# Chunked attention and a four-expert mixture: three groups of 1024 tokens in halves of 512 in place of four of 768, half expert steps, and an order searched over a moving stretch

## The chip, the cores and the metric

The kernel runs on one core of a Trainium2 chip. The metric is the device time of one execution in microseconds; before the change it was 1044.03 us (median of three runs, 1043.26 to 1044.74). Engines are named as in the profile: PE is the matrix engine, PEld its weight loads, DVE the vector, ACT the scalar and POOL the GpSimd engine; SP issues the DMAs.

## The reference, cut to what matters

Attention in chunks of 32 queries, each with 16 keys to the left, 8 to the right and 8 memory slots, is followed by four experts that all tokens visit; their results are weighed by normalised probabilities and added.

```python
B, H, S, D = 4, 8, 768, 64          # q, k, v; 3072 tokens of H * D = 512 in all
for c in range(S // 32):
    q_c = q[:, :, 32*c : 32*c+32]
    k_full = concat([mem_k, k[:, :, l:r]])      # l, r: 16 to the left, 8 to the right
    v_full = concat([mem_v, v[:, :, l:r]])
    a = exp(s - max(s)), s = q_c @ k_full.T / 8
    out[chunk] = a / (sum(a) + 1e-9) @ v_full
x = out.transpose(0, 2, 1, 3).reshape(3072, 512)
p = probs / (probs.sum(-1) + 1e-9)
for e in range(4):                   # w1: 512 x 1024, w2: 1024 x 512
    y += p[:, e] * (relu(x @ w1[e]) @ w2[e])
```

## The kernel before

**Number format.** A wide product is made of three matmuls in a 32-bit format that PE rounds (fp32r): each operand is split into a `hi` part, rounded by ACT, and a `lo` part, the rest, by DVE or POOL (`parts_of`). hi x hi, lo x hi and hi x lo are added in PSUM.

**Groups.** The 3072 tokens go through the experts in four groups of 768, in two halves of `SG` = 384 columns (one batch element each, b = 0 to 3); `n` = 4 b + e counts expert steps. Attention works on units of 96 queries, 8 to a group. The opening makes the units of the first group; those of the next group are strewn into the steps before it (`attend`, `window`). A unit has three pieces on PE: scores (`S`, L485), the turn of the probabilities (`T`, L1350, in the opening alone; later DVE transposes them in blocks, L661) and the product with v (`X`, L1369 and L618).

**The layers.** The first expert of the first group has plain products (`plain_first`, L817). All other first layers go by a scheme with seven products in place of eight (Strassen's, with sums of weight blocks and of token blocks made beforehand; `Pair`, `product`, L883): a pair p of blocks of 128 hidden rows takes the products 1, 2, 6, 5, 7, 4, 3 with SG columns and 6 matmuls each. There are four pairs to an expert (`NP2`). The second layer is made in three ways. Group 0 (`Tokens`, L863) multiplies 128 tokens with 512 columns of w2, eight hidden blocks of three matmuls to a bank. Group 1 (`Halves`, L1123) has the seven products with 256 columns. Groups 2 and 3 (`Across`, L1167) have the seven products with outputs across: 128 output features by 384 tokens, two strips, four pairs of three matmuls to a bank. After each bank, DVE (ACT the first time) adds it to an accumulator in SBUF (`add_up`, `join`).

**Weights.** While group 0 is worked on, the sums of w1 blocks (`make_pair`) and of w2 blocks (`make2_combined`, half of them later) are made and written to DRAM; from group 1 on, a ring of 9 buffers (`Stream`) reads them back, 30 transfers to an expert step. At a change of group, `combine_x` makes the sums of token blocks, 4 subtractions and 7 splits.

**Order.** Nothing is scheduled by the compiler. The program records operations with what they read and write (`Plan.add`); the order of PE is that in which they are recorded. The recorded order of the opening is the text `FIRST_BLOCK` (`W` n: n idle matmuls that keep PE's clock up, `S` u, `T` u, `X` u: unit u; `M` f, `N` f: hidden block f for the first units or for the rest of the half; `g`, `G`: a token tile's second layer). There are three plans: opening, group 0 (`plan.run(ahead=LEAD)`) and the rest. `Plan.run` then orders the other engines in a list scheduler with due times: it tries `TURNS` shifts of due times over the whole plan, chooses between DVE and POOL (or ACT and DVE) where an operation has two ways, and keeps what its own cost formulas call shortest.

## Time and profile before

| | |
|---|---|
| reported time, median of 3 runs | 1044.03 us |
| profiled execution, first to last instruction | 1041.7 us |
| DVE busy | 809.4 us (78%), 1358 instructions |
| ACT busy | 539.3 us (52%), 1426 |
| POOL busy | 464.9 us (45%), 426 |
| DMA moved | 300.88 MB, mean 289 GB/s |
| granted PE clock | 0.997 of full speed on average |

Of the profiled execution only the span is recorded; the median of the three runs is 2.3 us above it. A row of the grouped view gives the busy time of a group and the mean of one instruction. For PE that mean is from issue to modelled end and overlaps the next matmul, so the rate of PE is read from long rows of the chain (time of the row divided by its count) or from start to start.

### The profile page before, as it was taken

Reading aid. Unit: us, or ns where it says so; the run is one execution under the profiler, and the core shown is the slowest. Engines: PE = TensorE matmul, PEld = TensorE weight load, DVE = VectorE, ACT = ScalarE, POOL = GpSimd, SP = SyncE. Lnnn points to the kernel's source line nnn. Section 1 sums busy time; section 2 is a strip of 40 time slices with the busy share of each in tenths; the row PEclk is TensorE's granted clock in tenths of the full one; section 3 lists DMA queues with packets and bytes.
Section 4 is the critical chain, followed back from the end, with each engine's and each line's share of the span. In section 5 each row is a group of like instructions: output and inputs, shape, how many; then the busy total and the mean of one; then the engine's idle time right before and its main releaser. Section 6 shows DMA issues by size and latency. Waiting matters only on the chain.

```text
span 1041.7 us, 21404 instructions
## 1 busy us (share of the span) xinstructions
PE 1030.7 (99%) x7899; PEld 988.8 (95%) x7899; DVE 809.4 (78%) x1358; ACT 539.3 (52%) x1426; POOL 464.9 (45%) x426
## 2 busy tenths in 40 slices
PE   7999999999999999999999999999999999999998
PEld 6988988989889999999999999999999999999998
DVE  6869786868976768678797968969699765949485
ACT  5636864746737656474755546445453534334241
POOL 2444654854605436172253606346072634626172
PEclk8999999999999999999999999999999999999999
DMA  9557989989979999999988878879679887879784
GB/s 297 179 206 238 376 335 359 357 333 352 347 279 384 357 306 333 326 342 328 309 259 303 282 259 278 279 246 296 232 241 305 287 262 247 280 237 275 250 253 144
DMA packets 185512, 300.88 MB, mean 289 GB/s; under 512 B 14816, under 2 KB 125504, under 8 KB 185408
## 3 DMA queue, kind: packets, MB, share of 16 engines
q1 hardware_dynamic: 185408, 299.51, 84.4%
q8 instruction: 63, 1.03, 0.4%
q14 instruction: 41, 0.34, 0.1%
HBM read 230.21 MB, written 69.26 MB: 287 GB/s over the span
## 4 chain that ended last, share of the span: by engine, by line
PE 93%; DVE 4%; DMA 1%; issue 1%; POOL 0%; ACT 0%; SPq 0%; DVEq 0%; POOLq 0%; ACTq 0%
PE a_ps L883 22%; PE moe_ps L883 16%; PE moe_ps L863 13%; PE a_ps L1167 12%; PE moe_ps L1167 10%; PE a_ps L1123 7%; PE moe_ps L1123 5%; PE moe_ps L817 3%; PE x_ps L618 2%; PE s_ps L485 2%; DVE A_lo L568 1%; DVE u L983 1%; DVE u L568 1%; DMA raw<-in_w_dram 1%; DMA qk_pair<-in_qk_dram 1%
## 5 line engine op out<-in xcount | busy, mean ns | idle before, releaser
L569 POOL TENSOR_TENSOR u<-u,routes 128x384 f32<-128x384 f32 x46 | 50.3, 1095 | 191.8 <-ACT u L552 191.5
L568 DVE TENSOR_TENSOR A_lo<-u,A_hi 128x384 fp32r<-128x384 f32 x139 | 118.2, 868 | 18.8 <-ACT A_hi L550 18.4
L863 PE MATMUL moe_ps<-w,h_hi 128*128 128x512 f32 x384 | 119.8, 393 | 0.0
L568 DVE TENSOR_TENSOR u<-moe_ps,u 128x384 f32<-128x384 f32 x120 | 66.2, 552 | 63.4 <-PE moe_ps L883 48.3
L569 POOL TENSOR_TENSOR raw<-raw 128x256 f32<-128x256 f32 x57 | 51.2, 899 | 127.1 <-DMA raw<-in_w_dram 83.1
L550 ACT COPY u<-a_ps 128x384 f32<-128x384 f32 x120 | 57.0, 475 | 78.8 <-PE a_ps L883 77.1
L550 ACT CAST A_hi<-u 128x384 fp32r<-128x384 f32 x144 | 73.3, 514 | 37.5 <-DVE u L983 31.1
L863 PEld LDWEIGHTS moe_ps<-w,h_hi 128*128 128x128 f32 x384 | 71.1, 188 | 14.8
L883 PE MATMUL a_ps<-xc_hi,ring 128*128 128x384 f32 x384 | 82.2, 336 | 0.0
L552 ACT ACTIVATE u<-u 128x384 f32<-128x384 f32 x96 | 50.2, 525 | 53.3 <-DVE u L568 52.7
L863 PE MATMUL moe_ps<-w,h_lo 128*128 128x512 f32 x192 | 75.0, 391 | 0.0
L569 POOL TENSOR_TENSOR us<-u,u 128x384 f32<-128x384 f32 x43 | 49.4, 1149 | 41.8 <-DVE u L983 20.3
L883 PEld LDWEIGHTS a_ps<-xc_hi,ring 128*128 128x128 f32 x384 | 67.8, 188 | 0.0
L1167 PE MATMUL a_ps<-A_hi,ring 128*128 128x384 f32 x256 | 65.8, 338 | 0.6 <-DVE u L983 0.6
L569 POOL TENSOR_TENSOR us<-u,us 128x384 f32<-128x384 f32 x43 | 49.5, 1151 | 30.2 <-DVE us L568 23.7
L569 POOL TENSOR_TENSOR u<-u,u 128x384 f32<-128x384 f32 x48 | 59.8, 1246 | 0.6
L569 POOL TENSOR_TENSOR u<-u,us 128x384 f32<-128x384 f32 x46 | 58.2, 1266 | 2.7 <-DVE A_lo L568 1.1
L639 ACT ACTIVATE s_sb<-s_ps,mx 96x64 f32<-96x64 f32 x192 | 57.1, 309 | 0.7
L568 DVE TENSOR_TENSOR acc<-a_ps,acc 128x384 f32<-128x384 f32 x52 | 28.8, 553 | 26.7 <-PE a_ps L1167 26.1
L883 PE MATMUL a_ps<-xc_lo,ring 128*128 128x384 f32 x192 | 48.9, 336 | 0.0
L1167 PEld LDWEIGHTS a_ps<-A_hi,ring 128*128 128x128 f32 x256 | 45.8, 188 | 2.4 <-DVE u L983 2.2
L569 POOL TENSOR_TENSOR w<-raw,w 128x512 fp32r<-128x512 f32 x25 | 35.9, 1443 | 26.7 <-ACT w L550 17.6
(237 smaller groups left out, 3110.8 us busy)
## 6 DMA issues: line engine op xcount, KB each, us to landing
ring<-k SPq DMA_DIRECT2D x144, 512.0 KB, 4.8
ring<-t SPq DMA_DIRECT2D x96, 512.0 KB, 6.0
ring<-w SPq DMA_DIRECT2D x72, 512.0 KB, 5.4
k<-w SPq DMA_DIRECT2D x48, 512.0 KB, 5.3
w<-w SPq DMA_DIRECT2D x32, 512.0 KB, 5.5
raw<-in_w_dram SPq DMA_DIRECT2D x62, 256.0 KB, 5.2
ring<-k SPq DMA_DIRECT2D x48, 256.0 KB, 4.1
qk_t<-in_qk_dram SPq DMA_DIRECT2D x24, 464.0 KB, 6.3
```

The source lines that it names most:

```text
L485: nc.tensor.matmul(s_ps.ap[c * CH:(c + 1) * CH, j * NPAIR + g, 0:KW], lhsT=x()[rows, g * UQ + c * CH:g * UQ + (c + 1) * CH], rhs=x()[rows, ...
L550: nc.scalar.copy(out(), x())
L552: nc.scalar.activation(out(), x(), func)
L568: ("DVE", t_dve(cols), lambda: nc.vector.tensor_tensor(out=out(), in0=x(), in1=y(), op=op)),
L569: ("POOL", t_pool(cols), lambda: nc.gpsimd.tensor_tensor(out=out(), in0=x(), in1=y(), op=op)),
L618: nc.tensor.matmul(x_out()[j * D:(j + 1) * D, g, :], lhsT=v_t.ap[:, h * D:(h + 1) * D], rhs=aT[:, j * NPAIR + g, :], start=True, stop=True,)
L639: now["plan"].add("ACT", t_act(KW) + 0.08, lambda h=h: nc.scalar.activation(s_sb.ap[:, h, :], s_in()[:, h, :], AF.Exp, bias=mx.ap[:, h, :] ...
L817: nc.tensor.matmul(ps.ap[:, lo:hi], lhsT=a[:, c * P:(c + 1) * P], rhs=x[:, c, lo:hi], start=(i == 0), stop=(i == len(steps) - 1),)
L863: nc.tensor.matmul(self.ps.ap, lhsT=h.ap[:, self.rows], rhs=w.ap[:, part, :], start=(i == 0 and k == 0), stop=(i == NF - 1 and k == 2),)
L883: nc.tensor.matmul(ps.ap[:, 0:SG], lhsT=a()[:, c * P:(c + 1) * P], rhs=y[:, k0 + c, :], start=(first and i == 0), stop=(i == len(steps) - ...
L1123: nc.tensor.matmul(ps.ap[:, cols], lhsT=x.ap[:, rows], rhs=w_ap[:, y, :], start=(begins and k == 0 and i == 0), stop=(k == NP2 - 1 and i = ...
L1167: nc.tensor.matmul(ps.ap[:, 0:SG], lhsT=w_ap[:, y, rows], rhs=x.ap, start=(begins and k == 0 and i == 0), stop=(k == NP2 - 1 and i == 2), ...
```

## The change

**Groups and halves.** `SG` becomes 512: three groups of 1024 tokens. A batch element and a unit no longer end where a group does: a unit of 96 can lie in two halves (`pieces`), and what belongs to the next group is kept in `xs` (`spilled`). The opening has 11 units in place of 8. `Halves` is gone: group 0 has token tiles, groups 1 and 2 are `Across`.

**Half steps.** An expert step is made in two parts of two pairs each (`part`): the seven products of two pairs, then the second layer over these pairs alone (`Across`: six matmuls to a bank, `Tokens`: four hidden blocks). So each output is added to its accumulator twice per expert. In `Across`, product 4 has a bank of its own and the bank of product 7 is added to two accumulators: 8 additions of 128 x 512 for each of two strips. Buffers of hidden rows (`HB`), second-layer weights (`W2B`) and sums (`ROOMS`, `SPLITS`) become fewer; the raw weights share five buffers; the ring takes 15 transfers to a half step. All `make2_combined` are within group 0.

**Order.** `MID` and `FIN` are texts like `FIRST_BLOCK` for half steps of group 0 and later. `run` searches over a stretch that moves on by 15 or 25 us of planned PE time, sees 40 to 120 us, and fixes what lies behind.

```diff
-SG = 384
+SG = 512
+GT = 2 * SG
+NG = N // GT
...
-HEAD = NU
-FLAT = 2
-FIRST_TURNS, FIRST_SEED = 600, 1
+HEAD = max(units_of(0)) + 1
+FLAT = 1
+HB, W1B, W2B = 9, 8, 6
+FIRST_TURNS, FIRST_SEED = 300, 1
 FIRST_BLOCK = """
-W32 S0 S1 S2 W6 S3 W30 T0 W6 X0 T1 W12 X1 S4 W12 M1 T3 M5 X3 M2 T2 S5 X2 S6 M6 N7 N5 N4 N6 N0 N2 T5 N1 N3 S7 X5
-g0 T4 g1 G0 X4 T7 G1 X7 T6 g2 X6 G2
+W32 S0 S1 S2 S3 W30 T0 W6 X0 W6 T1 X1 S4 W12 M1 T2 W12 S5 M0 X2 T3 T4 X3 S6 S7 M4 X4 T5 M5 X5 S8 N0 N1 T6 X6 N6
+T7 N3 N4 X7 S9 N7 N2 S10 T8 N5 g0 X8 g1 T9 g2 G0 X9 G1 T10 G2 X10 g3 G3
 """
-AHEAD = (0, 2, 2, 0, 0, 2, 2, 0)
+AHEAD = (2, 2, 0, 0, 2, 2, 0, 0)
...
+TURNS_MID, TURNS_FIN = 120, 200
+HOPS = {"first": (15.0, 40.0, 60.0), "mid": (25.0, 120.0, 40.0), "fin": (15.0, 80.0, 30.0)}
...
+        while place["at"] < len(self.line) or len(order) < len(ops):
+            t += hop
+            to, stop = bisect(births, t), bisect(births, t + sight)
...
+            place, copies, part = self.window(place, copies, to, stop, whole, turns * (2 if whole else 1), rng)
+            order += part
...
-RAWS = 3
+RAWS = 5
+ROOMS = {"11": 3, "22": 3, "12": 2, "21": 2, "s1": 2, "s2": 2}
+SPLITS = {"A11": 2, "A12": 2, "A22": 2, "Sa": 2, "Sb": 2}
+MID = """
+t A12 A6 A5 wA A7 A3 B12 A4 B6 @m wB B5 + B7 q0:2 C B4 B3 q1:3 + q0:3 q0 q1 @B q2 q3 N q4 q5 q6 X
+"""
+FIN = """
+A12 r30 r31 A6 A5 A7 B12 A4 B6 B5 B7 A3 @m B4 B3 c10 c40 c41 c20 c11 c21 c50 c51 c60 c61 S3 @B c70 X S4 c71
+"""
+PARTS = [KORDER[:NF // 2], KORDER[NF // 2:]]
...
-                f = KORDER[i]
+                f = self.fs[i]
...
-        INTO = {"1": ("a", 0, 0), "2": ("c", 0, 0), "6": ("a", 0, 1), "5": ("b", 1, 1),
-                "7": ("a", 1, 1), "4": ("a", 1, 0), "3": ("b", 0, 1)}
+        INTO = {"1": ("a", [(0, 0)]), "2": ("c", [(0, 0)]), "4": ("c", [(1, 0)]), "5": ("b", [(1, 1)]),
+                "6": ("a", [(0, 1)]), "7": ("a", [(1, 1), (1, 0)]), "3": ("b", [(0, 1)])}
...
-            for k in range(NP2):
-                w = self.stream.at[self.n, 2, right, k // 2]
-                hi, lo = self.k[k][left]
+            w = self.stream.at[self.n, 2, right, self.part]
+            last = len(self.k) - 1
+            for k, operands in enumerate(self.k):
+                hi, lo = operands[left]
...
+            for half, col in into:
+                key = self.n // E, half, 2 * col + t
...
+                    join(lambda o=o: o.ap, lambda: ps.ap[:, 0:SG], lambda o=o: o.ap, ALU.add, SG, [], [ps, o], psum=True)
```

Three places show what this moves. The first is PE in the opening, up to the first matmul over columns beyond the 192 of the first two units. Before (`L1350` is a turn, `L1369` a product with v, `L485` scores, `L817` the first layer with blocks `w`; two units of 96 make 192 columns, the half has 384):

```order
L1350 MATMUL att_ps<-ident,band_107 128x96 x8
L485 MATMUL att_ps<-qk_pair 32x64 x24
L1369 MATMUL x_ps<-aT_111,v_t 64x96 x8
L485 MATMUL att_ps<-qk_pair 32x64 x24
L817 MATMUL moe_ps<-xa_hi,w_441 128x192 x8
L817 MATMUL moe_ps<-xa_lo,w_441 128x192 x4
L817 MATMUL moe_ps<-xa_hi,w_398 128x384 x8
```

Now (`L1405`, `L1420`, `L581` and `L918` are the same operations):

```order
L1420 MATMUL x_ps<-aT_113,v_t 64x96 x8
L581 MATMUL att_ps<-qk_pair 32x64 x48
L918 MATMUL moe_ps<-xa_hi,w_408 128x192 x8
L918 MATMUL moe_ps<-xa_lo,w_408 128x192 x4
L1420 MATMUL x_ps<-aT_111,v_t 64x96 x8
L1405 MATMUL att_ps<-ident,band_109 128x96 x8
L918 MATMUL moe_ps<-xa_hi,w_423 128x192 x8
L918 MATMUL moe_ps<-xa_lo,w_423 128x192 x4
L1420 MATMUL x_ps<-aT_113,v_t 64x96 x8
L581 MATMUL att_ps<-qk_pair 32x64 x24
L918 MATMUL moe_ps<-xa_hi,w_384 128x320 x8
```

The first matmuls over the rest of the half came after the fourth product with v, and now come after the sixth. The second place is PE where one `Across` step ends and the first layer of the next begins. Before:

```order
L1167 MATMUL moe_ps<-Sb_hi,ring 128x384 x2
L1167 MATMUL moe_ps<-Sb_lo,ring 128x384
L883 MATMUL a_ps<-xc_hi,ring 128x384 x4
L883 MATMUL a_ps<-xc_lo,ring 128x384 x2
L883 MATMUL moe_ps<-xc_hi,ring 128x384 x4
L883 MATMUL moe_ps<-xc_lo,ring 128x384 x2
```

Now, at the end of a half step:

```order
L1224 MATMUL moe_ps<-Sb_hi,ring 128x512 x2
L1224 MATMUL moe_ps<-Sb_lo,ring 128x512
L984 MATMUL a_ps<-xc_hi,ring 128x512 x4
L984 MATMUL a_ps<-xc_lo,ring 128x512 x2
L984 MATMUL moe_ps<-xc_hi,ring 128x512 x4
L984 MATMUL moe_ps<-xc_lo,ring 128x512 x2
```

Each product has the same number of matmuls, and each matmul has 512 columns in place of 384. The third place is DVE near the end of a step's second layer in the last group (`acc` is an accumulator, `Sa` and `Sb` are the splits of the second layer's sums). Before:

```order
L568 TENSOR_TENSOR acc<-moe_ps,acc 128x384
L568 TENSOR_TENSOR Sa_lo<-u_10625,Sa_hi 128x384
L568 TENSOR_TENSOR Sa_lo<-u_10697,Sa_hi 128x384
L568 TENSOR_TENSOR Sa_lo<-u_10784,Sa_hi 128x384
L568 TENSOR_TENSOR Sa_lo<-u_10876,Sa_hi 128x384
L568 TENSOR_TENSOR Sb_lo<-u_10683,Sb_hi 128x384
L568 TENSOR_TENSOR Sb_lo<-u_10768,Sb_hi 128x384
L568 TENSOR_TENSOR Sb_lo<-u_10863,Sb_hi 128x384
L568 TENSOR_TENSOR Sb_lo<-u_10948,Sb_hi 128x384
L568 TENSOR_TENSOR acc<-a_ps,acc 128x384 x2
```

Now:

```order
L665 TENSOR_TENSOR acc<-moe_ps,acc 128x512
L665 TENSOR_TENSOR Sa_lo<-u_10150,Sa_hi 128x512
L665 TENSOR_TENSOR acc<-moe_ps,acc 128x512
L665 TENSOR_TENSOR acc<-a_ps,acc 128x512
L665 TENSOR_TENSOR u_10266<-u_10266,us_10319 128x512
L665 TENSOR_TENSOR acc<-a_ps,acc 128x512
L665 TENSOR_TENSOR Sb_lo<-u_10210,Sb_hi 128x512
L665 TENSOR_TENSOR acc<-a_ps,acc 128x512 x2
L665 TENSOR_TENSOR acc<-moe_ps,acc 128x512
L665 TENSOR_TENSOR acc<-a_ps,acc 128x512 x2
```

The splits that stood in one row of eight are strewn between additions, and there are more additions for the same number of splits.

More of the change, by code (lines that the diff above doesn't have):

```diff
@@ L1 @@
 import random
+from bisect import bisect
 from contextlib import ExitStack
@@ L220, in run @@
-        self.assign(state[1])
-        self.replay(best[1], 0)
-        for _, op in sorted(best[1], key=lambda x: (x[0], x[1].index)):
+        self.line = [op for op in ops if op.engine == "PE"]
+        self.noise = [[random.Random(s * 100003 + op.index).uniform(0.97, 1.06) for op in ops] for s in range(DRAWS)]
+        self.lands = [[random.Random(s * 100003 + op.index).uniform(0.2, 1.2) for op in ops] for s in range(DRAWS)]
+        self.bias, self.ways = [0.0] * len(ops), [0] * len(ops)
+        for op in ops:
+            op.put, op.left, op.ready = False, 0, 0.0
@@ new lines, in run, with judge @@
+        self.assign(self.ways)
+        free, dma, _, _, end = copies[0]
+        for op in ops:
+            op.end = end[op.index]
+        self.done = {**free, "DMA": dma}
+        self.score = self.judge([({**c[0], "DMA": c[1]}, max(c[4])) for c in copies])
+        self.emit(order)
+    def judge(self, ends):
+        total = 0.0
+        for free, most in ends:
+            if self.last:
+                total += most
+            elif not self.ahead:
+                total += free["PE"]
+            else:
+                total += max(free["PE"], free["SP"] + self.ahead, free["DMA"] + DMA_FIRST, *(free[e] - BEHIND for e in ("ACT", "DVE", "POOL")))
+        return total / len(ends)
@@ L266, in pushed @@
             for _ in range(rng.randrange(2, 14)):
-                need = [d for d in op.deps if d.engine != "PE"]
+                need = [d for d in op.deps if d.engine != "PE" and d in start]
                 if not need:
@@ L1140, in go @@
[L1140 to L1150 removed]
+            kind, into = self.INTO[name]
             begins = kind == "c" or (kind, t) not in self.banks
@@ L1580, in tile_chunked_attention_moe @@
+    for word in FIN.split():
+        if word[0] == "r":
+            rest.go(word[1], int(word[2]))
     with tc.manual_schedule():
-        plan.run(last=True)
+        plan.run("fin", TURNS_FIN, last=True)
 _INS = ["qk", "v", "probs", "w1", "w2"]
```

644 lines of the change are left out of this document (319 added, 325 removed).

## The prediction

> **What bounds the kernel now.** I read the page first, then PE by lines, then long rows of the chain, then windows by stage. The page's busy times, the row of PE in 40 slices, the granted clock and the chain of waits by engine:
>
> ```profile
> PE 1030.7 (99%) x7899; PEld 988.8 (95%) x7899; DVE 809.4 (78%) x1358; ACT 539.3 (52%) x1426; POOL 464.9 (45%) x426
> ...
> PE   7999999999999999999999999999999999999998
> ...
> PEclk8999999999999999999999999999999999999999
> ...
> PE 93%; DVE 4%; DMA 1%; issue 1%; POOL 0%; ACT 0%; SPq 0%; DVEq 0%; POOLq 0%; ACTq 0%
> ```
>
> PE is busy in every slice but the first and the last, at full clock, and 93% of the chain is PE. Four stages (opening's end and group 0; then groups 1, 2, 3), with the columns PE, PEld, DVE, ACT, POOL, clock, DMA:
>
> ```profile
> 75.00:300.00 225.00, 225.00 (x1626) 201.35 (x1625) 184.91 (x312) 137.75 (x385) 121.62 (x118) 1.00 0.89 331
> 300.00:585.00 285.00, 284.96 (x2434) 279.85 (x2433) 222.39 (x387) 170.45 (x481) 121.53 (x113) 1.00 0.94 321
> 585.00:835.00 250.00, 249.69 (x1776) 245.69 (x1774) 206.48 (x341) 121.55 (x334) 109.43 (x92) 1.00 0.83 270
> 835.00:1042.00 207.00, 202.93 (x1164) 201.47 (x1164) 140.58 (x215) 73.86 (x157) 86.12 (x74) 1.00 0.76 243
> ```
>
> After 75 us PE hardly waits, though DVE is at 78 to 83% in the first three. So time is the sum of PE's matmuls, and a search for a better order has almost no wait left to take away; it can only keep new waits out. I cost it at nothing by itself.
>
> **Rate of a matmul by its columns.** Rows of the chain (start, time, line, count) for 512 columns twice, then 256, 384, 384:
>
> ```profile
> 149.84 12.69 PE moe_ps L863 x56
> ...
> 209.95 17.91 PE moe_ps L863 x78
> ...
> 349.89 2.88 PE a_ps L1123 x24
> ...
> 869.58 2.08 PE a_ps L883 x12
> ...
> 895.82 8.32 PE moe_ps L1167 x48
> ```
>
> Per matmul: 226.6 and 229.6 ns; 120.0; 173.3; 173.3. From 256 to 384 columns it grows by 53.3 ns, 0.417 ns a column, so 13.3 ns are fixed, and 512 columns should take 226.7: the first row does. The second row has pieces just behind a change of tile.
>
> The Trainium skill ("TensorE: Matmul & The Clock Gate", section "Back-to-back issue gap") speaks against this: it gives N / 2.4 + 2.5 ns, thus 109, 162.5 and 216 ns, a fixed part of 2.5 ns alone. The rows are 10.8 ns above it at each width, so the trace does not agree; what it would make of the change is a rival below.
>
> **Term A, the matmuls.** Counts of lines L883, L1167, L1123, L863, L817 in this order, from windows over the whole span:
>
> ```profile
> 0.00:1042.00 1042.00, 448.21 (x2520) 1.00 0.85 289
> ...
> 0.00:1042.00 1042.00, 238.11 (x1344) 1.00 0.85 289
> ...
> 0.00:1042.00 1042.00, 124.00 (x1008) 1.00 0.85 289
> ...
> 0.00:1042.00 1042.00, 135.87 (x576) 1.00 0.85 289
> ...
> 0.00:1042.00 1042.00, 37.35 (x240) 1.00 0.85 289
> ```
>
> Before: 2520 + 1344 and 144 of L817 make 4008 of 384 columns, 694.7 us; 1008 of 256, 121.0; 576 of 512 at the slower 229.6, 132.2; 96 of L817 with 192 columns, about 0.12 each (25.91 to 26.87 for eight, below), 11.5. Sum 959.4 us.
>
> After, from the loops: first layers 11 steps x 4 pairs x 42 = 1848; `Across` 8 x 7 x 2 x 4 x 3 = 1344; `Tokens` 4 x 8 x 8 x 3 = 768; plain 144 of 512, 48 of 320, 48 of 192. 3336 of 512 at 226.7 make 756.3; the 768 at 229.6, 176.3; 48 at 146.7 (on the same line), 7.0; 48 at 0.12, 5.8. Sum 945.4. **A = -14.0**: 1488 matmuls less, worth 19.8 us, against 15,360 columns more (256-column seven-product steps give way to plain ones), worth 6.4; the rest comes from the 192-column ones, of which half are left. If all 512-column matmuls ran at 229.6 it would be 955.0, so A lies between -4 and -14.6 (all at 226.7, before too); I take -14 because the 384-column rows of the same products lie on the line exactly.
>
> **Term B, attention on PE.** Pieces of a unit (turn, scores, product):
>
> ```profile
> 45.24 0.66 PE att_ps L1350 x8
> ...
> 49.35 0.67 PE att_ps L485 x46
> 50.02 0.81 PE x_ps L1369 x16
> ```
>
> All 32 units keep scores and product; three more are turned on PE: 3 x 0.66, **B = +2.0**. DVE loses their block transposes.
>
> **Term C, the opening.** DVE's split of the first and of the fourth unit's output, then PE from twelve idle matmuls over the first `M` to the first `N` (start, time):
>
> ```profile
> 20.23 0.56 DVE L1377 TENSOR_TENSOR xa_lo<-x_ps,xa_hi 128x384 fp32r<-128x384 f32 x1 [1.57 <-PE x_ps L1270]
> ...
> 33.77 0.55 DVE L1377 TENSOR_TENSOR xa_lo<-x_ps,xa_hi 128x384 fp32r<-128x384 f32 x1
> ```
> ```profile
> 22.38 0.83 PE L1270 MATMUL x_ps<-idle 128*128 128x128 bf16 x12
> 23.03 1.11 PE L817 MATMUL moe_ps<-xa_hi,w 128*128 128x192 f32 x8
> ...
> 25.91 1.11 PE L817 MATMUL moe_ps<-xa_hi,w 128*128 128x192 f32 x8
> 26.87 0.61 PE L817 MATMUL moe_ps<-xa_lo,w 128*128 128x192 f32 x4
> ...
> 34.80 0.37 PE L817 MATMUL moe_ps<-xa_hi,w 128*128 128x384 f32 x1
> ```
>
> Three units take DVE 13.5 us, 4.5 each. Before, PE has from 23.0 to 34.8 four `M` (5.8), two turns, two products, two scores (4.3): 10.1 of 11.8, idle 1.7. Now a half needs six units: DVE gives the sixth at 20.2 + 5 x 4.5 = 42.8, the first `N` at 43.4. Until then PE has four `M` (5.8), four turns (2.6), four products (3.2), three scores (2.0), 12 idle matmuls (0.7): 14.3, ready at 37.3. Idle 6.1, that is 4.4 more. Afterwards PE has 38 us of work (48 x 0.1467 + 96 x 0.2267 of layers, 9.4 of attention) against DVE's 5 x 4.5 = 22.5, so nothing is added. **C = +4.** Below it is 0, if DVE's order feeds PE in time. Above, the slice of the opening where PE waited most:
>
> ```profile
> 10.00:20.00 10.00, 7.64 (x115) 6.89 (x101) 7.43 (x13) 6.27 (x14) 1.51 (x1) 0.70 0.94 273
> ```
>
> Idle 24% and clock 0.70 over 20 us would be 4.7 + 4.3, so +9.
>
> **Term D, the end.** The last row of the chain:
>
> ```profile
> 1038.30 0.56 DVE acc L568
> ```
>
> This addition takes 0.19 more at 4/3 the columns, and the store behind it is larger: **+0.3**.
>
> **Terms E and F, new waits on DVE.** Groups of instructions (busy, mean ns):
>
> ```profile
> L568 DVE TENSOR_TENSOR A_lo<-u,A_hi 128x384 fp32r<-128x384 f32 x139 | 118.2, 868 | 18.8 <-ACT A_hi L550 18.4
> ...
> L568 DVE TENSOR_TENSOR acc<-a_ps,acc 128x384 f32<-128x384 f32 x52 | 28.8, 553 | 26.7 <-PE a_ps L1167 26.1
> ...
> L568 DVE TENSOR_TENSOR raw<-raw,t_hi 128x512 fp32r<-128x512 f32 x30 | 24.3, 810 | 3.5 <-ACT t_hi L550 3.3
> ...
> L568 DVE TENSOR_TENSOR xr<-xr 128x768 f32<-128x768 f32 x14 | 15.5, 1105 | 0.2
> ...
> L568 DVE TENSOR_TENSOR w<-s_t,w 128x512 fp32r<-128x512 f32 x15 | 13.9, 927 | 3.3 <-ACT w L550 3.3
> ...
> L568 DVE TENSOR_TENSOR xc_lo<-xr,xc_hi 128x768 fp32r<-128x768 f32 x10 | 11.9, 1203 | 0.0
> ```
>
> In the second layer of a half step PE has 14 products of 6 x 0.2267, 19.0 us. DVE has 16 additions (553 x 4/3 = 0.74) and about seven splits and sums (0.81 to 0.93, say 0.87): 17.9, or 94%. Banks wait for the additions, and behind them in DVE's queue stand the splits that PE needs next. Two windows of 20 us show what that is worth so far:
>
> ```profile
> 880.00:900.00 20.00, 20.00 (x116) 19.71 (x116) 19.93 (x27) 7.63 (x17) 18.28 (x16) 1.00 0.84 265
> 900.00:920.00 20.00, 20.00 (x117) 20.00 (x117) 11.74 (x21) 4.57 (x9) 2.73 (x3) 1.00 0.83 262
> ```
>
> DVE is full for 20 us without a wait of PE, then has 8 us to spare: a backlog is worked off. In a half step the first-layer part (about 15 of 19 us) has that room too. **F = +1** for 16 half steps, from -1 to +8 (0.5 a half step).
>
> At a change of group DVE has three subtractions and two splits more (3 x 1.47 + 2 x 1.60 = 7.6), 25.5 in all; PE has 19.0 and the next four products, 24.5: 1 us late. Two such changes, the first out of token tiles with half the additions: **E = +1.5**, 0 to +5. POOL's larger share of splits and ACT's fewer instructions hide behind PE (45 and 52% now). The ring reads 15 transfers per half step (168 x 0.2267 = 38 us) where it read 30 per step (336 x 0.1733 = 58 us), so DMA (0.76 to 0.94 busy above) gets lighter; it was hidden already, so this brings nothing.
>
> **Sum.** -14 + 2 + 4 + 0.3 + 1 + 1.5 = -5.2: span 1036.5; with the 2.3 us by which the median lies above the span, **1038.8, say 1039 us**. A measurement here can tell about 0.2% (2.1 us) from no change, thus 1041.9 and 1046.1 are the bounds.
>
> **Rivals.**
> - *DVE becomes the bound in half steps* (slower). If the seven splits take 868 x 4/3 = 1.16 us, as the contended `A_lo` does, DVE has 19.9 us against 19.0. It decides from 1.03 us each, if the first-layer part does not make up for it. For it: 94%; shorter steps leave less room to lag. Against: the two windows. Price 16 x 0.95 = 15 on top of the sum: 1054.
> - *The opening eats the gain* (no change): C at +9, the rest as it stands: 1044.
> - *No new wait at all*: C, E, F at 0: 1032.
> - *Fixed cost of 2.5 ns* (slower): if 10.8 of the 13.3 ns went with the layout of these products and not with the count, 1488 matmuls less would save 3.7 us against 6.4 of columns, A = +2.7: 1055. This is the skill's formula; rows of three widths are against it.
>
> **Chances.** Forecast 0.50 (1034 to 1044; 0.44 faster, 0.06 same); DVE 0.20, slower; opening 0.15 (0.12 same, 0.03 slower); no wait 0.13, faster; 2.5 ns 0.02, slower. Faster 0.57, same 0.18, slower 0.25. The range 1031 to 1054 leaves out part of the DVE case and of the best one.
>
> **What would show it.** A: rows of 12 matmuls of 512 columns at 2.72 us. C: the first matmul of 320 columns near 43 us. E: PE idle before the first products of groups 1 and 2. F: PE's idle time before second-layer products, with `Sa_lo` or `acc` as what ended it, under 0.1 us a half step. Wrong if 512 columns take 230 ns or more, if PE's busy share falls below 98% after 90 us, or if the opening ends (first `xb` product) later than 88 us.

## The result, and the profile after

The changed kernel takes 1081.15 us (median of four runs, 1080.57 to 1081.92) against 1044.32 for the kernel before in the same runs: 1.0352 times as long, with an interval of 1.0338 to 1.0367. The forecast was 1039, in a range of 1031 to 1054: wrong in sign and outside the range. One of the four runs of e10 below, the one with the trace, took 1129.92 us at a granted clock of 0.85; e10's ratio leaves it out, and only counts are read from its trace.

The page of the changed kernel: the span, busy times of the engines, the row of PE in 40 slices, the granted clock, and the chain by engine:

```profile
span 1079.0 us, 17724 instructions
...
PE 1050.9 (97%) x6435; PEld 841.3 (78%) x6435; DVE 839.1 (78%) x1250; ACT 493.4 (46%) x1155; POOL 513.9 (48%) x403
...
PE   7899999999999999999999999998999999999998
...
PEclk8999999999999999999999999999999999999999
...
PE 83%; DVE 11%; issue 2%; ACT 1%; DMA 1%; POOL 1%; DVEq 0%; POOLq 0%; ACTq 0%
```

PE has 1464 matmuls less and is busy 20 us longer. The chain now is DVE for 11%, where it was 4%. POOL works 49 us more. The granted clock is nearly as before (0.993 in the mean, 0.997 before).

Three stages from 90 us on (group 0, group 1, group 2 with the end; columns as in the prediction):

```profile
90.00:430.00 340.00, 337.21 (x2129) 271.74 (x2128) 264.71 (x423) 182.33 (x484) 149.47 (x145) 1.00 0.82 293
430.00:745.00 315.00, 307.41 (x1822) 242.89 (x1821) 262.56 (x383) 143.15 (x375) 158.27 (x108) 0.99 0.65 201
745.00:1079.00 334.00, 325.89 (x1379) 257.94 (x1377) 246.32 (x322) 118.48 (x198) 170.53 (x112) 1.00 0.60 186
```

PE stands still for 18.5 of 989 us, the end's 4 us included; before, for next to nothing up to the end. That is too little for 37 us. Most of the rest is in PE's own rate. Rows of the chain (start, time, line, count):

```profile
153.95 2.81 PE a_ps L984 x12
...
170.99 16.54 PE moe_ps L964 x72
...
1056.72 4.22 PE moe_ps L1224 x18
```

Per matmul of 512 columns these are 234.2, 229.7 and 234.4 ns; in the second row all but the first five start 226 to 227 ns apart. The prediction took 226.7, read from token tiles (now L964) and from 384 columns; L984 and L1224, first and second layer products, are 3192 matmuls at 234.

Where PE waited, and for what (total, times, longest):

```profile
PE a_ps L1224 <- DVE Sb_lo L665: 3.8, 3, 2.6
PE a_ps L1224 <- issue: 2.5, 3, 1.5
PE att_ps L581 <- issue: 2.2, 2, 1.6
PE att_ps L581 <- DVE s_sb L1360: 1.9, 2, 1.3
PE a_ps L984 <- ACT u L647: 1.9, 2, 1.1
```

Before, the list ended after seven rows and 7.4 us, nearly all in the opening; now it has 20 rows and 24.1 us.

**An account of PE's time.** The times from one matmul's start to the next, over the whole trace, were sorted into four parts: what the matmuls of the layers cost at 226.7, 173.3, 146.7, 120.0 and 111.1 ns for 512, 384, 320, 256 and 192 columns; what each took beyond that up to 0.2 us (rate); what went beyond by more (waits); and attention with the idle matmuls and their waits. From the first start to the last, in us:

| | before | after | e1 | e3 | e5 | e16 |
|---|---|---|---|---|---|---|
| layers at nominal | 956.6 | 942.5 | 942.5 | 942.6 | 942.5 | 942.5 |
| rate | 9.1 | 35.6 | 12.4 | 35.3 | 12.3 | 37.3 |
| waits of the layers | 2.3 | 16.8 | 23.2 | 4.9 | 7.6 | 28.6 |
| attention, idle matmuls | 68.9 | 78.8 | 81.0 | 78.4 | 79.4 | 77.0 |

After against before: -14.1 + 26.5 + 14.5 + 9.9 = 36.8. (e1 to e16 are experiments below. The 15.8 us of waits in some expectations are the same waits after 90 us, counted from a slightly higher threshold; here they are 16.8.)

### The profile page after: what moved, and what is told of

Same layout as the page of the kernel before. It is cut to its first block, busy times and chain, and to the rows that moved or that the text cites. A ratio compares the mean times of both kernels' runs of the same rounds, so it can differ in the third digit from the quotient of the medians.

```text
span 1079.0 us, 17724 instructions
## 1 busy us (share of the span) xinstructions
PE 1050.9 (97%) x6435; PEld 841.3 (78%) x6435; DVE 839.1 (78%) x1250; ACT 493.4 (46%) x1155; POOL 513.9 (48%) x403
## 4 chain that ended last, share of the span: by engine, by line
PE 83%; DVE 11%; issue 2%; ACT 1%; DMA 1%; POOL 1%; DVEq 0%; POOLq 0%; ACTq 0%
PE a_ps L984 22%; PE moe_ps L984 16%; PE moe_ps L964 14%; PE moe_ps L1224 12%; PE a_ps L1224 10%; PE moe_ps L918 3%; DVE acc L665 1%; PE x_ps L723 1%; DVE u L665 1%; DVE A_lo L665 1%; PE s_ps L581 1%; DVE Sb_lo L665 1%; DVE us L665 1%; DVE aT L771 1%; PE x_ps L1420 1%
## 5 line engine op out<-in xcount | busy, mean ns | idle before, releaser
L964 PE MATMUL moe_ps<-w,h_hi 128*128 128x512 f32 x512 | 159.3, 392 | 0.0
L666 POOL TENSOR_TENSOR A_lo<-u,A_hi 128x512 fp32r<-128x512 f32 x43 | 61.5, 1435 | 193.9 <-ACT A_hi L647 193.8
L647 ACT COPY u<-a_ps 128x512 f32<-128x512 f32 x88 | 51.7, 587 | 132.5 <-PE a_ps L984 131.5
L964 PEld LDWEIGHTS moe_ps<-w,h_hi 128*128 128x128 f32 x512 | 95.2, 188 | 20.5
L964 PE MATMUL moe_ps<-w,h_lo 128*128 128x512 f32 x256 | 99.8, 390 | 0.9 <-DVE h_lo L904 0.9
L665 DVE TENSOR_TENSOR u<-moe_ps,u 128x512 f32<-128x512 f32 x88 | 60.5, 687 | 46.0 <-PE moe_ps L984 22.5
L665 DVE TENSOR_TENSOR acc<-moe_ps,acc 128x512 f32<-128x512 f32 x120 | 80.2, 683 | 11.4 <-PE moe_ps L1224 8.8
L665 DVE TENSOR_TENSOR acc<-a_ps,acc 128x512 f32<-128x512 f32 x120 | 78.8, 681 | 6.5 <-PE a_ps L1224 4.8
L647 ACT CAST A_hi<-u 128x512 fp32r<-128x512 f32 x96 | 59.4, 622 | 48.7 <-DVE u L1084 44.1
L1224 PE MATMUL moe_ps<-A_hi,ring 128*128 128x512 f32 x256 | 80.7, 396 | 0.0
L984 PE MATMUL a_ps<-xc_hi,ring 128*128 128x512 f32 x256 | 70.4, 397 | 1.1 <-ACT u L647 1.1
L665 DVE TENSOR_TENSOR A_lo<-u,A_hi 128x512 fp32r<-128x512 f32 x53 | 50.2, 951 | 18.9 <-ACT A_hi L647 18.3
L984 PEld LDWEIGHTS a_ps<-xc_hi,ring 128*128 128x128 f32 x256 | 48.1, 188 | 13.3 <-ACT u L647 1.6
L1224 PEld LDWEIGHTS moe_ps<-A_hi,ring 128*128 128x128 f32 x256 | 48.2, 188 | 11.8
L964 PEld LDWEIGHTS moe_ps<-w,h_lo 128*128 128x128 f32 x256 | 48.1, 188 | 11.5 <-DVE h_lo L904 1.3
L1224 PE MATMUL moe_ps<-A_lo,ring 128*128 128x512 f32 x128 | 51.0, 399 | 0.1
```

The costliest lines, as they stand in the source:

```text
L647: nc.scalar.copy(out(), x())
L665: ("DVE", t_dve(cols), lambda: nc.vector.tensor_tensor(out=out(), in0=x(), in1=y(), op=op)),
L666: ("POOL", t_pool(cols), lambda: nc.gpsimd.tensor_tensor(out=out(), in0=x(), in1=y(), op=op)),
L964: nc.tensor.matmul(self.ps.ap, lhsT=h.ap[:, self.rows], rhs=w.ap[:, part, :], start=(i == 0 and k == 0), stop=(i == len(self.fs) - 1 and k ...
L984: nc.tensor.matmul(ps.ap[:, 0:SG], lhsT=a()[:, c * P:(c + 1) * P], rhs=y[:, k0 + c, :], start=(first and i == 0), stop=(i == len(steps) - ...
L1224: nc.tensor.matmul(ps.ap[:, 0:SG], lhsT=w_ap[:, y, rows], rhs=x.ap, start=(begins and k == 0 and i == 0), stop=(k == last and i == 2), ski ...
```

## The experiments

Theory for the rate: it depends on where the two operands lie in SBUF. Rivals: the values they hold, or a stationary operand that is used twice in a row, as in the token tiles. Theory for the waits: the search makes them. Rival: the half steps do, since DVE has too little slack there.

### m1: the rate by address alone

A kernel of streams, with the start bytes as parameters:

```diff
+ for cols in (512, 384, 256):
+     for moving in (0, 8, 16, 24):          # float32 elements, 32 bytes apart in steps of 8
+         for fixed in (0, 8, 16, 24):
+             stream(cols, moving, fixed)    # 42 matmuls, lhsT=w[:, b + fixed ...], rhs=x[:, a + moving ...]
+ stream(512, 0, 0, zeros, zeros)
...
```

> Nothing of the reference is computed: streams of fp32r matmuls alone, 42 to a stream in groups of 6 on one bank, for 512, 384 and 256 columns, with the first byte of the moving operand at 0, 32, 64 or 96 modulo 128 and that of the stationary one at 0, 32, 64 or 96; then streams of 512 columns with zeros as one operand, with a stationary operand used twice in a row, and with 12 matmuls on a bank. In the changed kernel the 512-column matmuls of lines 918, 984 and 1224 start 234.3 ns apart (moving at 0, stationary at 96), those of line 964 226.7 ns (moving 96, stationary 96). Theory 1, addresses: the pair (0, 96) gives 234 +- 1 and the pair (96, 96) 227 +- 1 in 512 columns, and 384 columns give 173.3 at (0, 96). Theory 2, what the operands hold or how a stationary one is used: all sixteen pairs agree within 1 ns, and zeros or the doubled use give 227 where the others give 234. Theory 3, something around the stream (DMA, other engines, the length of the run): all streams here give 226.7.

The sixteen pairs do not agree, and one operand of zeros (233.3 ns at distance 224, 234.3 at 96) or a doubled use (233.3 at 224, 232.1 at 128) gives what plain data gives at the same distance; so it is neither data nor doubled use. Nor do the pairs go by each operand alone. Sorted by the distance from moving to stationary start byte, modulo 256, they do. Mean ns from start to start, last 28 of each stream:

| distance | 0 | 32 | 64 | 96 | 128 | 160 | 192 | 224 |
|---|---|---|---|---|---|---|---|---|
| 512 columns | 226.7 | 233.3 | 233.3 | 234.3 | 232.4 | 233.2 | 228.9 | 233.3 |
| 384 columns | | 173.4 | 174.7 | 173.3 | 175.7 | 176.7 | 173.3 | 176.6 |
| 256 columns | | 118.1 | 113.3 | 117.3, 120.0 | 119.1 | 120.0 | 117.8 | 117.8 |

Pairs with one distance agree within 0.4 ns but for 256 columns at 96 and 128. Distance 0 was run once, with zeros in both operands, so m1 alone does not tell distance from zeros there; the kernels' token tiles and e1 have that distance with data. Windows over two streams, distance 96 and then 0 (42 starts each):

```profile
54.46:64.29 9.83, 9.83 (x43) 7.91 (x42) 0.00 (x0) 0.00 (x0) 0.00 (x0) 1.00 0.01 2
388.54:398.11 9.57, 9.57 (x44) 7.88 (x42) 0.00 (x0) 0.00 (x0) 0.00 (x0) 1.00 0.01 2
```

9.83 / 42 = 234.0 and 9.57 / 42 = 227.9 ns, the start of the stream included, with no other engine or DMA at work. By the programs' addresses, L984, L1224 and L918 of the changed kernel are at distance 96, L964 at 0; in the kernel before, the 384-column lines are at 96, L1123 at 160, L863 at 0. Each has the rate of its column in this table. So 384 columns were at one of their best distances, and 512 columns came to their worst.

### e1 and e2: the distance alone, in both kernels

e1, the changed kernel:

```diff
     psum_e = const.tile([P, NT, 1], F32, name="psum_e")
+    const.tile([P, 40], F32, name="shift")
...
-        lambda: late["sb"], [P, width + (72 if "fin" in late else 0)], "qk_t", 1)
+        lambda: late["sb"], [P, width + (32 if "fin" in late else 0)], "qk_t", 1)
```

> The changed kernel with 160 bytes laid behind the last tile of the first pool and a pad of the scores' tile cut by 160 bytes: every 512-column matmul then has its stationary operand at 0 modulo 256 from its moving one (before: 96), by the start bytes; nothing else differs, the order on each engine neither. Theory 1, rate by distance of the two operands: the stream of the two zero operands in the first run had 226.7 ns at distance 0 and those at 96 had 234.3; so lines 918, 984 and 1224 go to a median of 227 and 3336 x 7.6 ns = 25 us fall away: 1056. Theory 2, zeros were what made it fast: 234 stays, 1081. Rival to the first: DVE comes to bound, the waits take back some, 1062 to 1070.

1065.35 us, 1.0202 times the kernel before (1.0186 to 1.0217). Groups of matmuls of the changed kernel and then of e1, whose lines are one further (busy, mean ns from issue to modelled end):

```profile
L1224 PE MATMUL moe_ps<-A_hi,ring 128*128 128x512 f32 x256 | 80.7, 396 | 0.0
L984 PE MATMUL a_ps<-xc_hi,ring 128*128 128x512 f32 x256 | 70.4, 397 | 1.1 <-ACT u L647 1.1
```
```profile
L1225 PE MATMUL moe_ps<-A_hi,ring 128*128 128x512 f32 x256 | 78.8, 389 | 0.0
L985 PE MATMUL a_ps<-xc_hi,ring 128*128 128x512 f32 x256 | 68.6, 390 | 1.2 <-ACT u L648 1.2
```

The same order of the same instructions, 7 ns a matmul apart, and a median of 227 ns from start to start. The rate part of the account falls by 23.2 us, near the 25 expected; the time falls by 15.8 only, into the range of the rival, since waits grow by 6.4 and attention by 2.2. A faster PE shows more of what it waits for.

e2, the kernel before:

```diff
-            lambda: late["sb"], [P, width + (72 if "fin" in late else 0)], "qk_t", 1)
+            lambda: late["sb"], [P, width + (112 if "fin" in late else 0)], "qk_t", 1)
```

> The kernel before, with the pad of the scores' tile made 160 bytes longer, so that the distance of stationary from moving operand goes from 96 to 192 in line 1167 (384 columns) and from 160 to 64 in line 1123 (256 columns). The first run had 113.3 ns for 256 columns at 64 and 120.0 at 160, and 173.3 for 384 columns at both 96 and 192. Theory 1: line 1123 goes to 113.3, 1008 x 6.7 ns = 6.8 us less, 1037; nothing at 384 columns. Theory 2 (distance means nothing in the full kernel): 1044.

1041.85 us, 0.9978 times (0.9968 to 0.9988), faster than both kernels. L1123 goes from 120.8 to 117.4 ns in the mean, 3.4 us in all and half of what was expected, and the time falls by 2.2; its matmuls start 113 to 118 ns apart. Why it does not settle at 113.3 stays open.

### e3: the search over the whole plan at once

```diff
-HOPS = {..., "mid": (25.0, 120.0, 40.0), "fin": (15.0, 80.0, 30.0)}
+HOPS = {..., "mid": (1e6, 1e6, 40.0), "fin": (1e6, 1e6, 30.0)}
-TURNS_MID, TURNS_FIN = 120, 200
+TURNS_MID, TURNS_FIN = 50, 50
```

The tries are doubled where a stretch is the whole plan: 100.

> The changed kernel with the search over the whole plan at once, as before, for its second and third part (100 tries each) in place of the moving stretch. Matmuls have not changed, so about 1081 less what the stretch costs. After 90 us PE stands still for 16 us in 19 waits of over 0.2 us, before the change for under 3. If the moving stretch makes these waits: 1068 to 1072. If it takes waits away, as it is meant to: 1085 or more. If waits come from the half steps whatever the order: 1079 to 1083.

1070.37 us, 1.0252 times (1.0235 to 1.0269): 10.8 us less, with the same groups, half steps and matmuls. Its page and stages:

```profile
PE 1047.9 (98%) x6435; PEld 840.9 (79%) x6435; DVE 858.3 (80%) x1289; ACT 494.2 (46%) x1155; POOL 453.3 (42%) x364
```
```profile
90.00:430.00 340.00, 340.00 (x2144) 274.89 (x2143) 263.62 (x417) 185.50 (x494) 153.18 (x152) 1.00 0.83 295
430.00:745.00 315.00, 312.03 (x1846) 246.46 (x1844) 275.11 (x417) 144.45 (x372) 129.46 (x85) 1.00 0.67 206
```

In group 0 PE does not wait at all, and in group 1 for 3.0 us where it was 7.6. DVE is busier than in the changed kernel and POOL less: 39 instructions went back to DVE. So, with PE at 234 ns, DVE's load in the half steps is not what stops it.

### e10 and e15: the search alone, on the kernel before

```diff
-        plan.run(ahead=LEAD)
+        plan.run("mid", TURNS_MID, ahead=LEAD)
-        plan.run(last=True)
+        plan.run("fin", TURNS_FIN, last=True)
...
```

The class `Plan` is that of the changed kernel as a whole, which differs from the old one also in how it finds stalls and weighs an order; the opening keeps 600 tries over its whole plan.

> The kernel before with one part of the change alone: the planner that searches over a moving stretch, for its second and third part (120 and 200 tries a stretch); tiles, groups, products and the opening's order are those of before. The prediction costed the search at nothing by itself, since PE hardly waited. Theory 1 (the longer search fits its own model, moves work to POOL, and the chip pays): more instructions on POOL, waits of PE of 5 to 15 us where there were 1 us, 1049 to 1060. Theory 2 (only the half steps, with their longer operations, are open to it): 1041 to 1046.

1.0150 times the kernel before (1.0126 to 1.0173), some 15.7 us. One part of the change alone, the one costed at nothing, loses about as much as the waits of the changed kernel come to. POOL has 501 instructions, 75 more.

e15 takes from it the search's right to move a sum between DVE and POOL:

```diff
-                ways = self.moved(self.ways, free_ops, rng)
+                ways = self.ways if self.last or self.ahead else self.moved(self.ways, free_ops, rng)
```

> The kernel before with the moving search alone, and no moves between DVE and POOL; with moves it was 1060.4, and had 485 rows on POOL, against 381 here and 396 in the kernel before. Theory 1 (work on POOL): 1044 to 1049. Theory 2 (tight order): 1054 to 1060.

1.0112 times (1.0071 to 1.0153): between the two theories. Its interval overlaps that of e10, so it is not shown that the moves cost anything here; with as many instructions on POOL as before (426) most of the loss stays.

### e4, e7, e8, e12, e16: what in the search

All are the changed kernel with one edit to its planner. e4, what it believes of DVE beside POOL (in both places):

```diff
-                time += 0.9 * min(pool_to - start, time)
+                time += pool_to - start
```

> The changed kernel, where the planner believes that a DVE operation with two operands in SBUF that starts while POOL works waits until POOL is done, in place of at most 0.9 of its own time more. In the trace after, such DVE operations that alone take 0.69 to 1.2 us took 5.23, 3.73, 3.00, 2.89, 2.82, 2.63 us while POOL went from one operation to the next without a gap, and five of the largest waits of PE (2.75, 1.09, 1.08, 1.03, 0.78) end behind them. If these are the cause of the waits and the planner can avoid them: 5 to 8 us less, 1073 to 1076. If not: 1079 or more.

e7, a longer sight:

```diff
-HOPS = {..., "mid": (25.0, 120.0, 40.0), "fin": (15.0, 80.0, 30.0)}
+HOPS = {..., "mid": (25.0, 300.0, 1e6), "fin": (15.0, 300.0, 1e6)}
```

> The changed kernel; the moving stretch of the second and third part sees 300 us of the plan and every operation behind it, not 120 and 80 us. Theory 1 (work on POOL): the search moves as much work to POOL as before and nothing is gained, 1076 to 1084. Theory 2 (the stretch is cut too short, so that what is late behind its end is pushed into the next): the waits at the start of group 1 and between the groups shrink, 1070 to 1074.

e8, the edit of e15 in the changed kernel:

> The changed kernel and its moving search, but in the second and third part the search may not move a sum or a split between DVE and POOL; it only reorders. POOL then has some 65 instructions less. The kernel with the search over the whole plan (1070.4) has 364 instructions on POOL against 403, none of its DVE operations with two SBUF operands takes over 2.5 us, where six do in the changed kernel (to 5.23), and PE's waits after 90 us nearly vanish. Theory 1, too much work put on POOL starves DVE: no DVE operation over 2.5 us, 1069 to 1074. Theory 2, the moving stretch orders everything so tightly that any delay is seen, whichever engine has it: waits stay, 1078 or more.

e12, slack at each handoff:

```diff
-        lag = {e: LATENCY_PE if e == "PE" else LATENCY for e in ENGINES}
+        lag = {e: (LATENCY_PE if e == "PE" else LATENCY) + (0.0 if name == "first" else 0.4) for e in ENGINES}
```

> The changed kernel with its moving search; in the second and third part the planner takes 0.4 us more from the end of an operation to the start of one on another engine that waits for it (0.52 and 0.6 in place of 0.12 and 0.2). Engine choice stays free (POOL keeps about as many rows). Theory 2, the search leaves no slack at the handoffs and any delay of the chip becomes a wait of PE: most of the 15.8 us of waits after 90 us go, 1068 to 1073. Theory 1, work on POOL is what matters: 1077 or more.

e16, another seed:

```diff
-        plan.run("mid", TURNS_MID, ahead=LEAD)
+        plan.run("mid", TURNS_MID, seed=2, ahead=LEAD)
-        plan.run("fin", TURNS_FIN, last=True)
+        plan.run("fin", TURNS_FIN, seed=2, last=True)
```

> The changed kernel with another seed of its moving search in the second and third part (2 in place of 1), and nothing else. How far the time goes from 1081.2 shows how much an order that the search holds for as good differs on the chip. If the eleven us of e3 come from the moving stretch itself: 1077 to 1085. If they are luck of one order: 1070 to 1076, or over 1086.

| | e8 | e3 | e7 | e4 | e12 | after | e16 |
|---|---|---|---|---|---|---|---|
| median, us | 1075.8 | 1070.4 | 1072.9 | 1084.9 | 1084.7 | 1081.2 | 1092.0 |
| times before | 1.0302 | 1.0252 | 1.0276 | 1.0384 | 1.0392 | 1.0352 | 1.0458 |
| interval from | 1.0280 | 1.0235 | 1.0254 | 1.0369 | 1.0374 | 1.0338 | 1.0441 |
| to | 1.0324 | 1.0269 | 1.0297 | 1.0400 | 1.0411 | 1.0367 | 1.0476 |
| waits of the layers after 90 us | 10.7 | 4.7 | 8.6 | 14.8 | 17.3 | 16.8 | 28.2 |
| products with a broadcast operand on POOL | 0 | 2 | 2 | 5 | 8 | 9 | 11 |
| sums of 1024 columns on POOL | 0 | 2 | 6 | 6 | 5 | 7 | 11 |

Slack did not help (e12), so the theory that the order is only too tight has no support here. A longer sight (e7) came out as its second theory has it, that the stretch is cut too short; e8 lies between its two. e4, which raises the planner's price of a meeting, is not faster, so that this price is what misleads the search is not shown. Another seed (e16) costs 11 us more, above the 1086 put down for luck of one order: e3's gain is of the size by which two orders of one search differ, and alone does not show that the moving stretch is at fault. The last two rows are counts from the traces. The four kernels with five or more of those products on POOL are the four slowest, the three with two or none the three fastest. What these operations do to DVE is the next point.

### m2 and m3: DVE beside POOL

The longest wait of PE, 2.58 us, in the changed kernel: DVE's row at 484 us, POOL's rows, and PE's.

```profile
483.16 6.23 DVE L665 TENSOR_TENSOR Sb_lo<-us,Sb_hi 128x512 fp32r<-128x512 f32 x2
```
```profile
483.64 1.50 POOL L666 TENSOR_TENSOR s_sb<-s_sb,sm 96x512 f32<-96x512 f32 x1
485.10 1.29 POOL L666 TENSOR_TENSOR u<-u,u 128x512 f32<-128x512 f32 x1
486.35 1.27 POOL L666 TENSOR_TENSOR u<-u,us 128x512 f32<-128x512 f32 x1
487.58 1.27 POOL L666 TENSOR_TENSOR Sa_lo<-u,Sa_hi 128x512 fp32r<-128x512 f32 x1
```
```profile
489.45 0.50 PE L1224 MATMUL a_ps<-Sb_lo,ring 128*128 128x512 f32 x1 [2.58 <-DVE Sb_lo L665]
```

Two splits that take 0.69 us each alone take 6.23; the second is held until POOL's row of four ends. Six DVE operations took over 2.5 us (5.23, 3.73, 3.00, 2.89, 2.82, 2.63); in the kernel before one did. Two of the six stand behind such a product on POOL, four behind a sum of 1024 columns. After five of the six PE has a wait of 0.78 to 2.75 us, counted from start to start as in the account (6.7 in all). m2 is sums alone, one on DVE that comes while POOL is in the first of several:

```diff
+ nc.scalar.copy(s0, b); nc.scalar.copy(s1, b)
+ for i in range(4): nc.gpsimd.tensor_tensor(out=g[i], in0=s0, in1=b, op=ALU.add)
+ nc.vector.tensor_tensor(out=d[0], in0=s1, in1=b, op=ALU.add)
```

> Nothing of the reference is computed: sums of 128x512 float32 on DVE and POOL alone, six times in each case: DVE alone, POOL alone, one of each at once, one DVE operation that comes while POOL is in the first of 1, 2, 4 operations, the same with one operand in PSUM, and four against four. In the changed kernel a DVE sum takes 0.69 us alone, 1.77 beside one POOL operation, and one took 5.23 where POOL went through four. Theory 1, a DVE operation of two SBUF operands that comes late waits until POOL has a gap: about 0.7 more than what is left of POOL's row, so 1.2 to 1.7 us behind one, 2.5 to 3 behind two and 5 to 5.7 behind four; 0.69 with an operand in PSUM. Theory 2, they share turn by turn: under 2 us in each case, and POOL's operations get longer.

```profile
78.72 5.37 POOL L33 TENSOR_TENSOR g<-s,b 128x512 f32<-128x512 f32 x4 [0.73 <-ACT s L30]
79.20 1.34 DVE L35 TENSOR_TENSOR d<-s,b 128x512 f32<-128x512 f32 x1 [4.76 <-ACT s L31]
```

Theory 2: DVE waits for the one operation that POOL is in, then has its turn, and POOL's next takes 1.71 in place of 1.26. With an operand in PSUM DVE takes 0.69 as alone. So four plain sums do not make 5.23. m3 puts on POOL what stood there, the product of the softmax by its reciprocal sums:

```diff
+ nc.gpsimd.tensor_tensor(out=g[0], in0=s0, in1=sm.broadcast_to([96, 8, 64]), op=ALU.mult)   # then three sums
```

> Nothing of the reference is computed: as the last run of sums on DVE and POOL alone, now with what stood on POOL where DVE waited longest in the changed kernel: one operation of 1024 columns (2.85 us there), and rows of three or four that begin with the product of 96 partitions by a broadcast operand. DVE's sum comes while POOL is in its first operation. Theory 1, DVE waits for the one operation that POOL is in, whichever it is: up to 2.5 to 3 us behind 1024 columns and under 1.8 behind each row. Theory 2, behind the broadcast product DVE does not get its turn until POOL's row ends: 3.3 to 3.9 us behind three and 4.5 to 5.3 behind four, and under 1.8 behind four plain sums.

The product, DVE's sum that came in it, and POOL's three sums; then one sum of 1024 columns:

```profile
48.47 1.04 POOL L30 TENSOR_TENSOR g<-s,sm 96x512 f32<-96x512 f32 x1 [1.16 <-ACT s L39]
48.94 4.77 DVE L44 TENSOR_TENSOR d<-s,b 128x512 f32<-128x512 f32 x1 [1.08 <-ACT s L40]
49.47 3.69 POOL L35 TENSOR_TENSOR g<-s,b 128x512 f32<-128x512 f32 x3
```
```profile
10.00 2.34 POOL L35 TENSOR_TENSOR g<-s,b 128x1024 f32<-128x1024 f32 x1 [1.16 <-ACT s L39]
10.48 2.41 DVE L44 TENSOR_TENSOR d<-s,b 128x512 f32<-128x512 f32 x1 [1.08 <-ACT s L40]
```

Theory 2 to the number: 4.77 us behind a row of four that begins with the product, 3.28 behind three, each of six times; where a plain sum stands first and the product second, at most 1.34. So both kinds that the table counts hold DVE: the product until POOL has no more work, a sum of 1024 columns until it is done. The product differs from the plain sums in its operation, its 96 partitions and its broadcast operand; which of these does it is not shown. By the Trainium skill ("SBUF — State Buffer", section "Who interferes with whom") a DVE instruction with two SBUF inputs contends with a GpSimd instruction that reads SBUF, the ports that they share are locked exclusively, and issue order decides who blocks: 1.34 and 2.41 agree, 4.77 does not, since it outlasts three more instructions that came later. The kernel before has one such product on POOL, e10 thirteen.

This is not the whole of the waits: 6.7 of the 16.8 us in the changed kernel stand behind such long operations. e4 has two DVE operations of over 2.5 us, PE waits behind neither, and its waits come to 14.8 us; e8 has none, and 10.7 us of waits.

### e5, e6, e11, e13, e14: both corrections together

All have the distance of e1 and the whole-plan search; e5 with 100 tries, e6 with 400, e11 with 10, e13 with the slack of e12, e14 without moves. Beside the edits shown:

```diff
-TURNS_MID, TURNS_FIN = 120, 200
+TURNS_MID, TURNS_FIN = 50, 50
```

This is the line of e5, e13 and e14; e6 has 200 and 200, e11 has 5 and 5.

> The two parts found so far together: operands at distance 0 (alone 16 us less) and the search over the whole plan (alone 11 us less). If they add up, 1054. At distance 0 the rate should give 25 us, and the moving search gave 9 of them back in waits; with the better order less is given back: 1046 to 1051. If half steps have DVE as their bound once PE runs at 226.7 ns: 1056 or more.

> As the last, with 400 tries over the whole plan in place of 100. If more tries in the planner's model do harm, as in the moving search: slower than the last by 2 to 6 us and more instructions on POOL. If the model is good enough and tries help: 1 to 4 us faster than the last, 1043 to 1050.

> The changed kernel with operands at distance 0 and the search over the whole plan with 10 tries, where 100 gave 1050.6 and 400 gave 1055.8. If tries do harm throughout: 1044 to 1049. If 100 is about where the good of the first tries and the harm of the later ones balance: 1049 to 1054. If tries are needed: over 1055.

> The same 0.4 us more, with operands at distance 0 and the search over the whole plan with 100 tries (1050.6 without it). Theory 2: of the 7 us of waits after 90 us that are left there, half or more go, 1045 to 1048. Theory 1: 1049 to 1054.

> Operands at distance 0, search over the whole plan with 100 tries, and no moves between DVE and POOL in the second and third part. POOL has only seven rows less than in the one with moves (1050.6), so Theory 1 gives 1049 to 1052. Theory 2: only the order counts, within 2 us of 1050.6 too unless the order falls out otherwise; a gap of over 3 us in either direction shows how much two orders that the planner holds for equal can differ on the chip.

| | e5 | e11 | e6 | e14 | e13 |
|---|---|---|---|---|---|
| median, us | 1050.6 | 1054.4 | 1055.8 | 1058.2 | 1073.9 |
| times before | 1.0063 | 1.0102 | 1.0107 | 1.0138 | 1.0284 |
| interval from | 1.0042 | 1.0085 | 1.0081 | 1.0120 | 1.0255 |
| to | 1.0084 | 1.0119 | 1.0133 | 1.0156 | 1.0313 |
| waits of the layers after 90 us | 7.4 | 11.7 | 11.0 | 9.0 | 28.7 |
| broadcast products, sums of 1024 on POOL | 2, 2 | 1, 1 | 2, 4 | 0, 0 | 4, 1 |

e5 is 30.6 us faster than the changed kernel, four more than the 15.8 and 10.8 of its parts, and still 0.6% slower than the kernel before. Forty times the tries of e11 (e6) gain nothing over it, and the one with slack (e13) is the slowest, beyond either of its theories, with one DVE operation of 4.95 us behind a broadcast product. e14 is 7.6 us slower than e5: that far apart can two orders be that the planner holds for about equal. The four without slack are all faster than e1, which has the same distance and the moving stretch (1.0063 to 1.0138 against 1.0202). This, more than e3, speaks for searching the whole plan, or for fewer tries; the two were not separated.

## Why the prediction was wrong, by its own steps

**Term A, -14.0: the count was right, the rate was not.** The matmuls at nominal are 14.1 us less. The step that failed is its bound, "If all 512-column matmuls ran at 229.6 it would be 955.0, so A lies between -4 and -14.6". Measured, the first two rows of the account give -14.1 + 26.5 = +12.4. The line of 0.417 ns a column and 13.3 ns went through 256 columns at distance 160, 384 at 96 and 512 at 0; that the three fell on a line was chance (256 columns take 113.3 to 120.0 by their distance). The 229.6 ns in one of two rows was no sign of this: both rows are token tiles at distance 0, and in the slower one all but the first five and the last start 226 to 227 ns apart. The kernel before has no matmul of 512 columns at another distance, so its trace could not give the rate. e1 shows the term: with the distance undone, 23.2 of the 26.5 us are gone. By the Trainium skill ("TensorE: Matmul & The Clock Gate", section "Back-to-back issue gap") 512 columns take 215.8 ns by the formula, which it gives for an isolated matmul, and about 131 ns in a stream; no stream here shows less than 226.7, so the traces agree with neither. The rival made of the formula gave A = +2.7 and did not come to pass as it was written.

**The search, costed "at nothing by itself": wrong.** The prediction said that it "can only keep new waits out". e10 shows 15.7 us for it alone; e3 gets back 10.8, though one seed moves as much. It was weighed as if it knew the chip. It only knows its model, which gives DVE at most 0.9 of its own time more for a meeting with POOL; m3 shows 4.77 us for 0.69. That this error makes the loss is shown for the 6.7 us of waits behind long DVE operations at most, and e4 did not mend it. This way to lose, an order that is better only in the planner's terms, was not among the rivals.

**Terms E and F, +2.5 for the half steps and the changes of group: about right, where the search sees the whole plan.** In e3 the waits are 4.9 us, 2.6 more than before, but PE runs at 234 ns there; at the 227 ns of the forecast (e5) they are 5.3 more, twice the term and inside its bounds. In the changed kernel they are 14.5 more, and PE's waits before second-layer products (L1224) alone are 7.5 us in 16 half steps. So "F under 0.1 us a half step" failed, yet not by the mechanism of the rival *DVE becomes the bound*: in e3 DVE is busier and PE waits less, and e5 stays under the 1056 us put down for that bound.

**Terms B and C, +6: 4 us short.** Attention and idle matmuls take 9.9 us more. The first `N` was forecast at 43.4 us and the `xb` products before 88, and both came so:

```profile
43.32 1.45 PE L918 MATMUL moe_ps<-xa_hi,w 128*128 128x320 f32 x8
```
```profile
83.52 1.79 PE L918 MATMUL moe_ps<-xb_hi,w 128*128 128x512 f32 x7
```

The first was luck in part. PE from 23 us, about the first `M`, to the first `N`, in the changed kernel and before (stretch, length, PE busy and count, clock, DMA share, GB/s):

```profile
23.00:43.32 20.32, 17.06 (x350) 0.92 0.79 268
...
23.00:34.80 11.80, 10.89 (x196) 1.00 0.70 249
```

PE stood still for 3.3 us, not 6.1, and was busy for 17.1, not 14.3, at a granted clock of 0.92: two errors that cancel.

**Term D, +0.3:** from the last matmul's start to the end of the span it is 4.3 us where it was 3.8. Right within 0.2.

**The signs it named.** Rows of 12 matmuls take 2.81 and not 2.72 us, and 512 columns over 230 ns: both gave the error away. PE's busy share after 90 us is 98.1% (970.5 of 989), just on the side called right, though the waits of the layers there had grown from 1.1 to 16.8 us: that sign was too coarse.

**Open.** Why the distance of two addresses modulo 256 sets the rate, and why a broadcast product keeps DVE out. What makes the other 10 us of waits in the changed kernel, the 9 to 11 us in orders without any such product on POOL (e8, e14), and the 29 in e13. A version with the distance of e1 and the softmax product held on DVE was not tried. Of what ran, e2 alone beats both kernels.

## What to carry to other kernels

Read a matmul's rate from the operands that the change will use, not from another line of the same width: where two operands lie to each other in SBUF was worth 3% at 512 columns, and a pad of 160 bytes moved it. A search over a planner's model gets better at the model; try the search alone on the old kernel, and with more than one seed, before it is costed at nothing. The longest wait here was set by one meeting of two engines, which their mean busy shares do not show.

## What was not expected of the hardware

- Matmuls of 512 fp32r columns back to back start 226.7 to 234.3 ns apart by the distance of their operands modulo 256 bytes, those of 384 from 173.3 to 176.7, of 256 from 113.3 to 120.0, with no other engine at work (m1). One operand of zeros, or a stationary operand used twice in a row, changed nothing beyond that; distance 0 was run with zeros in both operands, and with data in e1, where the median is 227.
- A DVE sum with both operands in SBUF takes 0.69 us alone, 1.34 when it comes during a plain POOL sum of 512 columns, 2.41 during one of 1024, and 4.77 when it comes during a product of 96 partitions with a broadcast operand that three sums follow; with an operand in PSUM, 0.69 (m2, m3).
